# Two-layer cached-attention decode: issuing loads ahead of the projections that stood before them, and contiguous input and output transfers

## The chip, the cores and the metric

The kernel runs on one core of one Trainium2 chip. The metric is device time in microseconds (us) of that core. "Before" ran at a median of 2728.05 us over 12 runs (2727.2 to 2729.18).

## The reference, cut to what matters

```python
# B=2, one query token, D=576, H=32 heads, Dh=128, cache length Sk=16384, F=4608, all bf16
def A(x, k_cache, v_cache, wq, wo):
    q = (x @ wq).reshape(B, 1, H, Dh).transpose(0, 2, 1, 3)
    p = softmax(einsum("bhqd,bhkd->bhqk", q, k_cache) * Dh ** -0.5)
    o = einsum("bhqk,bhkd->bhqd", p, v_cache)
    return o.transpose(0, 2, 1, 3).reshape(B, 1, H * Dh) @ wo

def Bm(x, w1, w2, w3, w4):      # with S=1 the shifted half of this block is zero
    return x + gelu(layernorm(x) @ w3) @ w4

for layer in range(2):
    x = x + A(layernorm(x), K, V, wq, wo)
    x = x + Bm(layernorm(x), w1, w2, w3, w4)
```

Both layers read the same K and V cache: 64 (batch, head) units per layer, each with 4 MiB of K and 4 MiB of V. That is 1074 MB of the 1109 MB that the profile counts as read from HBM. The weights are the rest, 35 MB.

## The kernel before

The kernel streams K and V through SBUF. For a unit it transposes K tile by tile on TensorE (PE), multiplies by the unit's q, takes the exponential on ScalarE, and multiplies by V. q (`qT_sb`) of all heads is made before the units of a layer start, from the layer's normalized x and the weight wq. These are the parts that the change touches; cuts are marked.

```python
    xin = small.tile([P, NCH, B], A_x.dtype)
    xap = A_x.rearrange("b o d -> d (b o)")
    for kc in range(NCH):                     # one packet per element
        nc.sync.dma_start(xin[: rows[kc], kc, :], xap[kc * P : kc * P + rows[kc], :])
    # ... cut: cast into xT, layernorm, helpers
    xq_f, xq_bf = layernorm(xT[:])
    with tc.tile_pool(name="wq0", bufs=1) as wqpool:
        wq_sb = load_weight_chunked(wqpool, A_wq, H * Dh, tag="wq", engines=[nc.sync, nc.sync])
        qT_sb = q_projection(wq_sb, xq_bf)
    w3_sb = load_weight_chunked(const, B_w3, F, tag="w3", engines=[nc.gpsimd, nc.gpsimd])

    for layer in range(num_layers):
        with (tc.tile_pool(name=f"stream{layer}", bufs=1) as spool, ...):   # cut: six pools, per layer
            pend_k = {0: issue_k(0)}          # two DMAs of 2 MB, slots k0..k3 in turn
            pend_v = {0: issue_v(0)}          # two DMAs of 2 MB, slots v0..v3 in turn
            pend_k[1] = issue_k(1)
            for ui, (b, h) in enumerate(units):
                # issues V of unit ui+1 and K of unit ui+2, then:
                # ... cut: transposes, scores, exp, oT
            # wo in slots k0,k1,k2; w4 in k3,v0,v1; wq of the next layer in v2,v3,w0
            # ... cut: these loads, the output projection (wo), layernorm, MLP (w3, w4)
            if layer + 1 < num_layers:
                xq_f, xq_bf = layernorm(xT[:])
                # ... cut: q projection of the next layer
    xob = small.tile([P, NCH, B], out.dtype)
    nc.vector.tensor_copy(out=xob[:], in_=xT[:])
    for kc in range(NCH):                     # one packet per element
        nc.sync.dma_start(oap[kc * P : kc * P + rows[kc], :], xob[: rows[kc], kc, :])
```

The streaming pools of a layer open only after the q projection of that layer, and on memory that earlier pools held. So the first K and V of a layer wait for the q projection.

The softmax here doesn't subtract the row's maximum and nothing guards it: scores larger than these inputs give would overflow.

Of the kernel before, what the change touches and what calls it, by code (L numbers as in the profile page):

```python
# [8 lines left out]
F32 = mybir.dt.float32  # L9
BF16 = mybir.dt.bfloat16  # L10
# [7 lines left out]
def kernel(  # L18
# [40 lines left out]

    ident = const.tile([P, P], BF16)  # L60
# [6 lines left out]
    xin = small.tile([P, NCH, B], A_x.dtype)  # L67
    xap = A_x.rearrange("b o d -> d (b o)")
    with nc.allow_non_contiguous_dma(reason="tiny transposed load"):
        for kc in range(NCH):  # L70
            nc.sync.dma_start(xin[: rows[kc], kc, :], xap[kc * P : kc * P + rows[kc], :])  # L71
    for kc in range(NCH):
        nc.vector.tensor_copy(out=xT[: rows[kc], kc, :], in_=xin[: rows[kc], kc, :])
# [63 lines left out]

    xq_f, xq_bf = layernorm(xT[:])
    with tc.tile_pool(name="wq0", bufs=1) as wqpool:
        wq_sb = load_weight_chunked(wqpool, A_wq, H * Dh, tag="wq", engines=[nc.sync, nc.sync])  # L140
        qT_sb = q_projection(wq_sb, xq_bf)
    w3_sb = load_weight_chunked(const, B_w3, F, tag="w3", engines=[nc.gpsimd, nc.gpsimd])

    for layer in range(num_layers):
        R = const.tile([P, U], F32)
        oT_all = const.tile([P, U], F32)
        with (
            tc.tile_pool(name=f"stream{layer}", bufs=1) as spool,
            tc.tile_pool(name=f"kt{layer}", bufs=KT_BUFS) as ktpool,
            tc.tile_pool(name=f"sexp{layer}", bufs=2) as sexp,  # L150
            tc.tile_pool(name=f"psT{layer}", bufs=4, space=bass.MemoryType.PSUM) as psT,
            tc.tile_pool(name=f"psS{layer}", bufs=2, space=bass.MemoryType.PSUM) as psS,
            tc.tile_pool(name=f"psO{layer}", bufs=1, space=bass.MemoryType.PSUM) as psO,
        ):
            units = [(b, h) for b in range(B) for h in range(H)]
            kslot = [0]
            vslot = [0]

            def issue_k(u):
                bb, hh = units[u]  # L160
                kap = A_k_cache[bb, hh].rearrange("(p j) d -> p j d", p=P)
                tl = []
                for c in range(NKT):
                    knat = spool.tile(
                        [P, KT_J, Dh], BF16, tag=f"k{kslot[0] % KSLOTS}", bufs=1
                    )
                    kslot[0] += 1
                    nc.sync.dma_start(knat[:], kap[:, c * KT_J : (c + 1) * KT_J, :])
                    tl.append(knat)
                return tl  # L170

            def issue_v(u):
                bb, hh = units[u]
                vap = A_v_cache[bb, hh].rearrange("(p j) d -> p j d", p=P)
                tl = []
                for vc in range(NVT):
                    vt = spool.tile(
                        [P, VT_J, Dh], BF16, tag=f"v{vslot[0] % VSLOTS}", bufs=1
                    )
                    vslot[0] += 1  # L180
                    nc.sync.dma_start(vt[:], vap[:, vc * VT_J : (vc + 1) * VT_J, :])
                    tl.append(vt)
                return tl

            pend_k = {0: issue_k(0)}
            pend_v = {0: issue_v(0)}
            if len(units) > 1:
                pend_k[1] = issue_k(1)
            for ui, (b, h) in enumerate(units):
# [5 lines left out]
                if ui + 2 < len(units):  # L195
                    pend_k[ui + 2] = issue_k(ui + 2)
# [180 lines left out]
    with nc.allow_non_contiguous_dma(reason="tiny transposed store"):  # L377
        for kc in range(NCH):
            nc.sync.dma_start(oap[kc * P : kc * P + rows[kc], :], xob[: rows[kc], kc, :])
# [30 lines left out]
```

## Time and profile before

| what | before |
|---|---|
| median time | 2728.05 us |
| span of the profiled run | 2726.1 us |
| DMA rate inside both K/V streams | 428 GB/s |
| time per unit in the stream (start to start) | 20.0 us |
| first K issued | 42.75 us |
| PE start of layer 1, first unit | 1388.8 us |
| last cast of x to end of span | 20.1 us |

This is part 2 of the page of the kernel before: the span in 40 equal slices, the busy share of the 16 DMA engines in tenths (9 is 90% or more), and what they moved.

```profile
DMA  7999999999999999999879999999999999999984
GB/s 297 428 428 427 428 428 428 427 429 428 428 427 428 421 425 422 423 421 425 321 307 428 428 428 428 428 428 427 428 428 427 428 428 420 425 420 425 423 377 148
```

The DMA engines are full except at the two ends and at slices 20 and 21, the layer boundary. A kernel like this is shortened by removing DMA idle time or bytes; work on other engines counts only where it keeps DMA waiting. The next fence is the same kernel by chosen stretches. The columns are: stretch, its length, busy time of PE, weight loads, DVE, ACT and POOL, the granted PE clock, the DMA share and GB/s.

```profile
core 0: us, PE busy (x) PEld busy (x) DVE busy (x) ACT busy (x) POOL busy (x), PEclk, DMA share, GB/s
...
10.00:20.00 10.00, 0.00 (x0) 0.00 (x0) 0.34 (x2) 0.00 (x0) 0.00 (x0) 1.00 1.02 336
...
31.00:43.00 12.00, 9.89 (x156) 8.94 (x156) 0.22 (x1) 0.00 (x0) 0.00 (x0) 1.00 0.02 4
...
1363.00:1382.00 19.00, 15.09 (x276) 13.88 (x273) 2.53 (x16) 0.20 (x1) 0.00 (x0) 0.50 0.05 14
...
2686.00:2726.00 40.00, 16.61 (x343) 15.42 (x341) 2.49 (x13) 0.26 (x1) 0.00 (x0) 0.50 0.05 12
```

Three holes are seen: 12 us at the head, 19 us at the layer boundary and 40 us at the tail. In the first two no K or V moves while PE works on the q projection (in the head 156 of its matmuls, 9.9 us; at the boundary the end of the MLP comes before it). From 10 to 20 us the engines are busy and yet move only 336 GB/s. The timeline of the head (start, duration, engine, line, operation, output<-input, count, idle time before it and its releaser) shows why:

```profile
0.74 2.77 SPq L71 DMA_DIRECT2D xin<-in_A_x_dram  x5
...
20.71 0.16 DVE L73 CAST xT<-xin 64x2 f32<-64x2 bf16 x1 [2.46 <-DMA xin<-in_A_x_dram]
...
32.82 9.89 PE L127 MATMUL qT_ps<-ybf,t 64*128 64x2 bf16 x156 [2.10 <-DMA t<-in_A_wq_dram]
42.75 0.82 SPq L168 DMA_DIRECT2D knat<-in_A_k_cache_dram  x2
```

The 2.3 KB of x need 20 us to arrive, because each element is a packet of its own and these packets take turns with the large packets of w3. wq lies behind them in the same queue. K is issued after the q projection.

At the boundary and at the tail the timeline of before has:

```profile
1333.06 0.45 PE L298 MATMUL yT_ps<-oT_bf,wot 128*128 128x2 bf16 x11 [2.65 <-DMA wot<-in_A_wo_dram]
...
1336.84 0.43 PE L298 MATMUL yT_ps<-oT_bf,wot 128*128 128x2 bf16 x10 [3.33 <-DMA wot<-in_A_wo_dram]
...
1381.43 0.82 SPq L168 DMA_DIRECT2D knat<-in_A_k_cache_dram  x2
1381.44 0.23 DVE L372 CAST qT_sb<-qT_ps 128x64 bf16<-128x64 f32 x1 [10.16 <-PE qT_ps L364]
...
2706.05 0.18 DVE L375 CAST xob<-xT 128x10 bf16<-128x10 f32 x1
2706.25 2.65 SPq L379 DMA_DIRECT2D out_dram<-xob  x5
```

K of layer 1 is issued at the moment q is ready, and the span ends 20 us after the last cast. The view of DMA issues gives the store's time from issue to landing (last column):

```profile
out_dram<-xob SPq DMA_DIRECT2D x4, 0.5 KB, 17.1
```

### The profile page before, as it was taken

How to read it: one execution, taken by the hardware profiler on the slowest of the kernel's cores; microseconds unless marked ns; L12 is line 12 of the kernel's file. 1: busy time of each engine (PE TensorE's matmuls, PEld its weight loads, DVE VectorE, ACT ScalarE, POOL GpSimd, SP SyncE). 2: the span in 40 equal slices, each digit the busy share in tenths (PEclk: the TensorE clock that was granted, in tenths of full speed). 3: DMA queues.
4: the chain of work that ended last, by engine and by line, in shares of the span. 5: the costliest groups of instructions: out<-in, count | busy, mean ns of one | idle time of the engine just before them, and what ended most of it. 6: DMA issues, size and time to landing. Idle time of an engine off the chain costs nothing.

```text
span 2726.1 us, 108877 instructions
## 1 busy us (share of the span) xinstructions
PE 2334.9 (86%) x50564; PEld 2117.4 (78%) x50564; DVE 1042.6 (38%) x2268; ACT 1039.3 (38%) x2318; POOL 2.1 (0%) x8
## 2 busy tenths in 40 slices
PE   3888988889888888888779888888888988888884
PEld 3877877878778877887768877878888878887774
DVE  1343434434334343443224444343443434434341
ACT  1343443434334343443224434343443434434340
POOL 0000000000000000000000000000000000000000
PEclk9777777777777787777667877777777777878775
DMA  7999999999999999999879999999999999999984
GB/s 297 428 428 427 428 428 428 427 429 428 428 427 428 421 425 422 423 421 425 321 307 428 428 428 428 428 428 427 428 428 427 428 428 420 425 420 425 423 377 148
DMA packets 97287, 1115.54 MB, mean 409 GB/s; under 512 B 11008, under 2 KB 28416, under 8 KB 30144
## 3 DMA queue, kind: packets, MB, share of 16 engines
q1 hardware_dynamic: 96224, 1103.27, 96.0%
q8 instruction: 395, 6.47, 0.8%
q0 software_dynamic: 608, 5.31, 0.6%
q14 instruction: 60, 0.49, 0.0%
HBM read 1108.54 MB, written 0.00 MB: 407 GB/s over the span
## 4 chain that ended last, share of the span: by engine, by line
DMA 69%; PE 25%; DVE 2%; ACT 2%; issue 1%; SPq 0%; DVEq 0%
DMA knat<-in_A_k_cache_dram 67%; PE kT_ps L203 15%; PE S_ps L216 5%; PE oT_ps L243 2%; DVE ktT L208 2%; ACT ktT L210 2%; DMA t<-in_A_wq_dram 1%; DMA wot<-in_A_wo_dram 1%; PE hT_ps L316 1%; PE y_ps L342 0%; PE yT_ps L298 0%; PE qT_ps L364 0%; PE qT_ps L127 0%; ACT S_exp L230 0%; SPq L71 0%
## 5 line engine op out<-in xcount | busy, mean ns | idle before, releaser
L203 PE MATMUL kT_ps<-ident,knat 128*128 128x128 bf16 x16384 | 1628.2, 243 | 135.1 <-DMA knat<-in_A_k_cache_dram 134.7
L210 ACT COPY ktT<-kT_ps 128x384 bf16<-128x384 bf16 x2048 | 980.6, 479 | 1525.7 <-DVE ktT L208 1525.7
L208 DVE COPY ktT<-kT_ps 128x640 bf16<-128x640 bf16 x2048 | 1006.2, 492 | 881.7 <-PE kT_ps L203 775.6
L203 PEld LDWEIGHTS <-knat 128*128 128x128 bf16 x16384 | 1146.1, 108 | 143.4 <-DMA knat<-in_A_k_cache_dram 128.3
L216 PE MATMUL S_ps<-qT_sb,ktT 128*128 128x1 bf16 x16384 | 1008.9, 168 | 77.2 <-ACT ktT L210 59.1
L216 PEld LDWEIGHTS <-ktT 128*128 128x128 bf16 x16384 | 761.9, 100 | 266.6 <-ACT ktT L210 114.0
L243 PE MATMUL oT_ps<-S_exp,vt 128*128 128x1 bf16 x16384 | 459.4, 165 | 98.4 <-ACT S_exp L230 60.4
L243 PEld LDWEIGHTS <-vt 128*128 128x128 bf16 x16384 | 455.6, 102 | 112.2 <-issue 111.9
L251 DVE COPY oT_all<-oT_ps 128x1 f32<-128x1 f32 x128 | 20.3, 158 | 656.7 <-PE oT_ps L243 656.7
L230 ACT ACTIVATE S_exp<-S_ps 128x128 bf16<-128x128 f32 x128 | 35.5, 278 | 40.4 <-PE S_ps L216 40.4
L96 ACT ACTIVATE stat<-stat 1x2 f32<-1x2 f32 x4 | 0.8, 203 | 65.5 <-DVE stat L93 65.5
L230 ACT ACTIVATION_READ_ACCUMULATOR S_exp<-S_ps 128x1 f32 x128 | 24.8, 194 | 0.0
L298 PE MATMUL yT_ps<-oT_bf,wot 128*128 128x2 bf16 (+1 forms) x320 | 12.2, 170 | 14.5 <-DMA wot<-in_A_wo_dram 11.5
L316 PE MATMUL hT_ps<-ybf,t 128*128 128x2 bf16 (+1 forms) x360 | 22.7, 172 | 1.7 <-DVE ybf L110 1.7
L316 PEld LDWEIGHTS <-t 128*128 128x128 bf16 (+1 forms) x360 | 20.7, 106 | 3.7 <-issue 1.7
L298 PEld LDWEIGHTS <-wot 128*128 128x128 bf16 (+1 forms) x320 | 11.6, 114 | 15.2 <-DMA wot<-in_A_wo_dram 11.8
L81 PE MATMUL sum_ps<-x,ones_f 128*1 128x4 f32 (+1 forms) x40 | 1.8, 166 | 23.0 <-DVE x L78 23.0
L81 PEld LDWEIGHTS sum_ps<-x,ones_f 128*1 128x1 f32 (+1 forms) x40 | 1.3, 80 | 23.4 <-DVE x L78 23.2
L342 PE MATMUL y_ps<-hT_bf,w4t 128*128 128x2 bf16 (+1 forms) x360 | 12.9, 170 | 6.0 <-DVE hT_bf L337 4.0
L127 PE MATMUL qT_ps<-ybf,t 128*128 128x2 bf16 (+1 forms) x160 | 10.2, 173 | 9.1 <-DMA t<-in_A_wq_dram 9.1
L342 PEld LDWEIGHTS <-w4t 128*128 128x128 bf16 (+1 forms) x360 | 12.5, 114 | 6.4 <-issue 6.4
L127 PEld LDWEIGHTS <-t 128*128 128x128 bf16 (+1 forms) x160 | 9.1, 106 | 10.1 <-DMA t<-in_A_wq_dram 9.3
(46 smaller groups left out, 55.6 us busy)
## 6 DMA issues: line engine op xcount, KB each, us to landing
knat<-in_A_k_cache_dram SPq DMA_DIRECT2D x256, 2048.0 KB, 31.9
vt<-in_A_v_cache_dram SPq DMA_DIRECT2D x256, 2048.0 KB, 33.7
w4t<-in_B_w_dram SPq DMA_DIRECT2D x6, 1728.0 KB, 16.3
wot<-in_A_wo_dram SPq DMA_DIRECT2D x4, 1584.0 KB, 30.1
t<-in_B_w_dram POOLq DMA_DIRECT2D x1, 4608.0 KB, 16.0
t<-in_A_wq_dram SPq DMA_DIRECT2D x1, 4096.0 KB, 26.9
wot<-in_A_wo_dram SPq DMA_DIRECT2D x2, 1440.0 KB, 14.1
wqt<-in_A_wq_dram SPq DMA_DIRECT2D x2, 1408.0 KB, 15.9
```

Source lines behind the costliest of these rows:

```text
L81: nc.tensor.matmul(sum_ps[:, :], lhsT=ones_f32[: rows[kc], 0:1], rhs=x2[: rows[kc], kc, :], start=(kc == 0), stop=(kc == NCH - 1),)
L127: nc.tensor.matmul(qT_ps[:, h * B : (h + 1) * B], lhsT=wq_sb[: rows[kc], kc, h * Dh : (h + 1) * Dh], rhs=xq_bf[: rows[kc], kc, :], start=( ...
L203: nc.tensor.transpose(kT_ps[:, e, :], knats[j // KT_J][:, j % KT_J, :], ident[:])
L208: nc.vector.tensor_copy(out=ktT[:, 0:nsplit, :], in_=kT_ps[:, 0:nsplit, :])
L210: nc.scalar.copy(out=ktT[:, nsplit:EG, :], in_=kT_ps[:, nsplit:EG, :])
L216: nc.tensor.matmul(S_ps[:, j : j + 1], lhsT=ktT[:, e, :], rhs=qT_sb[:, ucol : ucol + 1], start=True, stop=True,)
L230: nc.scalar.activation(S_exp[:], S_ps[:], ACT.Exp, scale=EXP_SCALE, accum_out=R[:, ucol : ucol + 1],)
L243: nc.tensor.matmul(oT_ps[:, 0:1], lhsT=vt[:, jj, :], rhs=S_exp[:, jg : jg + 1], start=first, stop=(jg == NJ - 1),)
L251: nc.vector.tensor_copy(out=oT_all[:, ucol : ucol + 1], in_=oT_ps[:, 0:1])
L298: nc.tensor.matmul(yT_ps[: rows[c], :], lhsT=wot[:, h - h0, c * P : c * P + rows[c]], rhs=oT_bf[:, h * B : (h + 1) * B], start=(h == 0), s ...
L316: nc.tensor.matmul(hT_ps[:, g, :], lhsT=w3_sb[: rows[kc], kc, g * P : (g + 1) * P], rhs=xq2_bf[: rows[kc], kc, :], start=(kc == 0), stop=( ...
L342: nc.tensor.matmul(y2_ps[: rows[c], :], lhsT=w4t[:, g - g0, c * P : c * P + rows[c]], rhs=hT_bf[:, g, :], start=(g == 0), stop=(g == FG - 1),)
```

## The change

The intent is to let loads start as soon as their SBUF slots are free, and to move x and the output as whole rows.

- The streaming pools are opened once, before the first q projection. K0 and V0 are issued at the start; wq is loaded in three column chunks from ACT's queue into slots `v2`, `v3` and `w0`.
- wo and w4 are issued in the last unit of a layer, into slots that come free in that order.
- The next layer's K0 is issued after the output projection, V0 and K1 after the q projection in program order. SP waits only for their slots.
- x is loaded as two rows and transposed on PE; the output is transposed on PE and stored as two rows.
- A tile `pad` of 160 bytes per partition is allocated and set to zero. Nothing reads it.

```diff
+    pad = small.tile([P, 80], BF16)
+    nc.vector.memset(pad[:], 0.0)
...
-    xin = small.tile([P, NCH, B], A_x.dtype)
-        for kc in range(NCH):
-            nc.sync.dma_start(xin[: rows[kc], kc, :], xap[kc * P : kc * P + rows[kc], :])
+    xin = small.tile([B, D], A_x.dtype)
+    nc.sync.dma_start(xin[:], A_x.rearrange("b o d -> (b o) d"))
     for kc in range(NCH):
+        xin_ps = psm.tile([P, B], A_x.dtype, tag="m")
+        nc.tensor.transpose(xin_ps[...], xin[:, kc * P : ...], ident[:B, :B])
...
+    next_pend_k = {0: issue_k(0)}
+    next_pend_v = {0: issue_v(0)}
+    wq0_tags = [f"v{(NVT + i) % VSLOTS}" for i in range(NVT)] + ["w0", "w1"]
+    for i, (h0, h1) in enumerate(hgroups0):
+        t = spool.tile([P, NCH, c1 - c0], BF16, tag=wq0_tags[i], bufs=1, name=f"wq0t{i}")
+        nc.scalar.dma_start(t[:, 0:nfull, :], A_wq[0 : nfull * P, c0:c1].rearrange(...))
+        nc.scalar.dma_start(t[: rows[-1], NCH - 1, :], A_wq[(NCH - 1) * P : D, c0:c1])
...
+                if ui == nu - 1:
+                    stage_wo_w4()
...
+            if layer + 1 < num_layers:
+                next_pend_k = {0: issue_k(0)}          # after the output projection
...
+                next_pend_v = {0: issue_v(0)}          # after the q projection
+                next_pend_k[1] = issue_k(1)
...
-        for kc in range(NCH):
-            nc.sync.dma_start(oap[kc * P : kc * P + rows[kc], :], xob[: rows[kc], kc, :])
+        nc.tensor.transpose(xo_ps[:, kc, : rows[kc]], xob[...], ident[...])
+    nc.vector.tensor_copy(out=xo_sb[:], in_=...)
+    nc.sync.dma_start(out.rearrange("b o d -> (b o) d"), xo_sb[:])
```

More of the change, by code (lines that the diff above doesn't have):

```diff
@@ L66 @@
     nc.vector.memset(xT[:], 0.0)
-    xin = small.tile([P, NCH, B], A_x.dtype)
-    xap = A_x.rearrange("b o d -> d (b o)")
-    with nc.allow_non_contiguous_dma(reason="tiny transposed load"):
-        for kc in range(NCH):
-            nc.sync.dma_start(xin[: rows[kc], kc, :], xap[kc * P : kc * P + rows[kc], :])
-    for kc in range(NCH):
-        nc.vector.tensor_copy(out=xT[: rows[kc], kc, :], in_=xin[: rows[kc], kc, :])
+    xin = small.tile([B, D], A_x.dtype)
+    nc.sync.dma_start(xin[:], A_x.rearrange("b o d -> (b o) d"))
+    for kc in range(NCH):
+        xin_ps = psm.tile([P, B], A_x.dtype, tag="m")
+        nc.tensor.transpose(
+            xin_ps[: rows[kc], :], xin[:, kc * P : kc * P + rows[kc]], ident[:B, :B]
+        )
+        nc.vector.tensor_copy(out=xT[: rows[kc], kc, :], in_=xin_ps[: rows[kc], :])
     def layernorm(src, eps=1e-5):
@@ L136, in q_projection @@
         return qT_sb
-    xq_f, xq_bf = layernorm(xT[:])
-    with tc.tile_pool(name="wq0", bufs=1) as wqpool:
-        wq_sb = load_weight_chunked(wqpool, A_wq, H * Dh, tag="wq", engines=[nc.sync, nc.sync])
-        qT_sb = q_projection(wq_sb, xq_bf)
-    w3_sb = load_weight_chunked(const, B_w3, F, tag="w3", engines=[nc.gpsimd, nc.gpsimd])
+    spool = ctx.enter_context(tc.tile_pool(name="stream", bufs=1))
+    ktpool = ctx.enter_context(tc.tile_pool(name="kt", bufs=KT_BUFS))
+    sexp = ctx.enter_context(tc.tile_pool(name="sexp", bufs=2))
@@ new lines, with issue_k @@
+    psT = ctx.enter_context(tc.tile_pool(name="psT", bufs=4, space=bass.MemoryType.PSUM))
+    psS = ctx.enter_context(tc.tile_pool(name="psS", bufs=2, space=bass.MemoryType.PSUM))
+    psO = ctx.enter_context(tc.tile_pool(name="psO", bufs=1, space=bass.MemoryType.PSUM))
+    units = [(b, h) for b in range(B) for h in range(H)]
+    kslot = [0]
+    vslot = [0]
+    ktags_unit = {}
+    vtags_unit = {}
+    def issue_k(u):
+        bb, hh = units[u]
+        kap = A_k_cache[bb, hh].rearrange("(p j) d -> p j d", p=P)
+        tl = []
+        for c in range(NKT):
+            tg = f"k{kslot[0] % KSLOTS}"
+            ktags_unit.setdefault((kslot[0] // (NKT * len(units))) if False else u, []).append(tg)
+            knat = spool.tile([P, KT_J, Dh], BF16, tag=tg, bufs=1)
+            kslot[0] += 1
+            nc.sync.dma_start(knat[:], kap[:, c * KT_J : (c + 1) * KT_J, :])
+            tl.append(knat)
+        return tl
@@ new lines, in issue_v @@
+    def issue_v(u):
+        bb, hh = units[u]
+        vap = A_v_cache[bb, hh].rearrange("(p j) d -> p j d", p=P)
+        tl = []
+        for vc in range(NVT):
+            tg = f"v{vslot[0] % VSLOTS}"
+            vtags_unit.setdefault(u, []).append(tg)
+            vt = spool.tile([P, VT_J, Dh], BF16, tag=tg, bufs=1)
+            vslot[0] += 1
+            nc.sync.dma_start(vt[:], vap[:, vc * VT_J : (vc + 1) * VT_J, :])
+            tl.append(vt)
+        return tl
+    next_pend_k = {0: issue_k(0)}
@@ new lines @@
+    next_pend_v = {0: issue_v(0)}
+    HGRP0 = 11
+    hgroups0 = [(h0, min(H, h0 + HGRP0)) for h0 in range(0, H, HGRP0)]
+    wq0_tags = [f"v{(NVT + i) % VSLOTS}" for i in range(NVT)] + ["w0", "w1"]
+    wq0 = []
+    for i, (h0, h1) in enumerate(hgroups0):
+        c0, c1 = h0 * Dh, h1 * Dh
+        t = spool.tile([P, NCH, c1 - c0], BF16, tag=wq0_tags[i], bufs=1, name=f"wq0t{i}")
+        nfull = (NCH - 1) if rows[-1] != P else NCH
+        nc.scalar.dma_start(
+            t[:, 0:nfull, :], A_wq[0 : nfull * P, c0:c1].rearrange("(kc p) f -> p kc f", p=P)
+        )
+        if nfull != NCH:
+            nc.scalar.dma_start(t[: rows[-1], NCH - 1, :], A_wq[(NCH - 1) * P : D, c0:c1])
+        wq0.append((c0, c1, t))
@@ new lines @@
+    w3_sb = load_weight_chunked(const, B_w3, F, tag="w3", engines=[nc.gpsimd, nc.gpsimd])
+    xq_f, xq_bf = layernorm(xT[:])
+    qT_ps0 = psm.tile([P, U], F32, tag="m")
+    for (c0, c1, wqt) in wq0:
+        for h in range(c0 // Dh, c1 // Dh):
+            for kc in range(NCH):
+                nc.tensor.matmul(
+                    qT_ps0[:, h * B : (h + 1) * B],
+                    lhsT=wqt[: rows[kc], kc, h * Dh - c0 : (h + 1) * Dh - c0],
+                    rhs=xq_bf[: rows[kc], kc, :],
+                    start=(kc == 0),
+                    stop=(kc == NCH - 1),
+                )
@@ L144 @@
+    qT_sb = const.tile([P, U], BF16, tag="qT")
+    nc.vector.tensor_copy(out=qT_sb[:], in_=qT_ps0[:])
+    if len(units) > 1:
+        next_pend_k[1] = issue_k(1)
     for layer in range(num_layers):
@@ L146 @@
         oT_all = const.tile([P, U], F32)
-        with (
-            tc.tile_pool(name=f"stream{layer}", bufs=1) as spool,
-            tc.tile_pool(name=f"kt{layer}", bufs=KT_BUFS) as ktpool,
-            tc.tile_pool(name=f"sexp{layer}", bufs=2) as sexp,
-            tc.tile_pool(name=f"psT{layer}", bufs=4, space=bass.MemoryType.PSUM) as psT,
-            tc.tile_pool(name=f"psS{layer}", bufs=2, space=bass.MemoryType.PSUM) as psS,
-            tc.tile_pool(name=f"psO{layer}", bufs=1, space=bass.MemoryType.PSUM) as psO,
-        ):
-            units = [(b, h) for b in range(B) for h in range(H)]
-            kslot = [0]
-            vslot = [0]
-            def issue_k(u):
-                bb, hh = units[u]
-                kap = A_k_cache[bb, hh].rearrange("(p j) d -> p j d", p=P)
-                tl = []
-                for c in range(NKT):
-                    knat = spool.tile(
-                        [P, KT_J, Dh], BF16, tag=f"k{kslot[0] % KSLOTS}", bufs=1
-                    )
-                    kslot[0] += 1
-                    nc.sync.dma_start(knat[:], kap[:, c * KT_J : (c + 1) * KT_J, :])
-                    tl.append(knat)
-                return tl
-            def issue_v(u):
-                bb, hh = units[u]
-                vap = A_v_cache[bb, hh].rearrange("(p j) d -> p j d", p=P)
-                tl = []
-                for vc in range(NVT):
-                    vt = spool.tile(
-                        [P, VT_J, Dh], BF16, tag=f"v{vslot[0] % VSLOTS}", bufs=1
-                    )
-                    vslot[0] += 1
-                    nc.sync.dma_start(vt[:], vap[:, vc * VT_J : (vc + 1) * VT_J, :])
-                    tl.append(vt)
-                return tl
-            pend_k = {0: issue_k(0)}
-            pend_v = {0: issue_v(0)}
-            if len(units) > 1:
-                pend_k[1] = issue_k(1)
@@ new lines, with stage_wo_w4 @@
+        for _u in list(ktags_unit):
+            if _u > 1:
+                del ktags_unit[_u]
+        for _u in list(vtags_unit):
+            if _u > 0:
+                del vtags_unit[_u]
+        if True:
+            HGRP = 11
+            GGRP = 12
+            HGROUPS = [(h0, min(H, h0 + HGRP)) for h0 in range(0, H, HGRP)]
+            GGROUPS = [(g0, min(FG, g0 + GGRP)) for g0 in range(0, FG, GGRP)]
+            nu = len(units)
+            early_tags = []
+            wq_tags = []
+            wo_t = []
+            w4_t = []
+            def stage_wo_w4():
+                tags = ["w0"] + list(ktags_unit.get(nu - 2, [])) + list(vtags_unit.get(nu - 2, []))
+                tags += list(ktags_unit.get(nu - 1, []))
+                while len(tags) < len(HGROUPS) + len(GGROUPS):
+                    tags.append(f"x{len(tags)}")
+                wq_tags.extend(tags[len(HGROUPS) + len(GGROUPS) :] + list(vtags_unit.get(nu - 1, [])))
+                wq_tags.extend(["w1", "w2"])
+                for i, (h0, h1) in enumerate(HGROUPS):
+                    t = spool.tile([P, h1 - h0, D], BF16, tag=tags.pop(0), bufs=1, name=f"wot{i}")
+                    nc.sync.dma_start(
+                        t[:, :, :], A_wo[h0 * Dh : h1 * Dh, :].rearrange("(h d) f -> d h f", d=Dh)
+                    )
+                    wo_t.append((h0, h1, t))
+                for i, (g0, g1) in enumerate(GGROUPS):
+                    t = spool.tile([P, g1 - g0, D], BF16, tag=tags.pop(0), bufs=1, name=f"w4t{i}")
+                    nc.sync.dma_start(
+                        t[:, :, :], B_w4[g0 * P : g1 * P, :].rearrange("(g p) f -> p g f", p=P)
+                    )
+                    w4_t.append((g0, g1, t))
+            if next_pend_k is not None:
+                pend_k = next_pend_k
+                pend_v = next_pend_v
+            else:
+                pend_k = {0: issue_k(0)}
+                pend_v = {0: issue_v(0)}
+                if len(units) > 1:
+                    pend_k[1] = issue_k(1)
@@ L251 @@
                 nc.vector.tensor_copy(out=oT_all[:, ucol : ucol + 1], in_=oT_ps[:, 0:1])
-            HGRP = 11
-            GGRP = 12
-            wo_t = []
-            for i, h0 in enumerate(range(0, H, HGRP)):
-                h1 = min(H, h0 + HGRP)
-                t = spool.tile([P, h1 - h0, D], BF16, tag=f"k{i % KSLOTS}", bufs=1, name=f"wot{i}")
-                nc.sync.dma_start(
-                    t[:, :, :], A_wo[h0 * Dh : h1 * Dh, :].rearrange("(h d) f -> d h f", d=Dh)
-                )
-                wo_t.append((h0, h1, t))
-            w4_t = []
-            w4tags = [f"k{i}" for i in range(len(wo_t), KSLOTS)] + [f"v{i}" for i in range(VSLOTS)]
-            for i, g0 in enumerate(range(0, FG, GGRP)):
-                g1 = min(FG, g0 + GGRP)
-                t = spool.tile([P, g1 - g0, D], BF16, tag=w4tags[i], bufs=1, name=f"w4t{i}")
-                nc.sync.dma_start(t[:, :, :], B_w4[g0 * P : g1 * P, :].rearrange("(g p) f -> p g f", p=P))
-                w4_t.append((g0, g1, t))
             wq_next = None
             if layer + 1 < num_layers:
-                nqt = len(wo_t)
-                wqtags = (w4tags[len(w4_t) :] + [f"w{j}" for j in range(nqt)])[:nqt]
                 wq_next = []
-                for i, (h0, h1, _) in enumerate(wo_t):
+                for i, (h0, h1) in enumerate(HGROUPS):
                     c0 = h0 * Dh
                     c1 = h1 * Dh
-                    t = spool.tile([P, NCH, c1 - c0], BF16, tag=wqtags[i], bufs=1, name=f"wqt{i}")
+                    t = spool.tile(
+                        [P, NCH, c1 - c0], BF16, tag=wq_tags[i], bufs=1, name=f"wqt{i}"
+                    )
                     nfull = (NCH - 1) if rows[-1] != P else NCH
@@ L372 @@
                 nc.vector.tensor_copy(out=qT_sb[:], in_=qT_ps[:])
+                next_pend_v = {0: issue_v(0)}
+                next_pend_k[1] = issue_k(1)
     xob = small.tile([P, NCH, B], out.dtype)
     nc.vector.tensor_copy(out=xob[:], in_=xT[:])
-    oap = out.rearrange("b o d -> d (b o)")
-    with nc.allow_non_contiguous_dma(reason="tiny transposed store"):
-        for kc in range(NCH):
-            nc.sync.dma_start(oap[kc * P : kc * P + rows[kc], :], xob[: rows[kc], kc, :])
+    xo_ps = psm.tile([B, NCH, P], out.dtype, tag="m")
+    for kc in range(NCH):
+        nc.tensor.transpose(
+            xo_ps[:, kc, : rows[kc]], xob[: rows[kc], kc, :], ident[: rows[kc], : rows[kc]]
+        )
+    xo_sb = small.tile([B, D], out.dtype)
+    nc.vector.tensor_copy(
+        out=xo_sb[:], in_=xo_ps[:].rearrange("b c p -> b (c p)")[:, 0:D]
+    )
+    nc.sync.dma_start(out.rearrange("b o d -> (b o) d"), xo_sb[:])
 _INS = ['A_x', 'A_k_cache', 'A_v_cache', 'A_wq', 'A_wo', 'B_x', 'B_w1', 'B_w2', 'B_w3', 'B_w4']
```

## The prediction

> **What bounds the kernel now.** DMA, through nearly all of the span. The slice table shows the engines 90-100% busy at 428 GB/s in both K/V streams. The packet records give 19.8 us per (batch, head) unit of 8.39 MB on average; the timeline starts a unit every 20.0 us, because part of the engines finish late (at the end of each stream the DMA share falls to 0.5 for some 17 us before the last V lands). PE needs about 19.4 us where it does not wait for K, and waits for K 1.4 us per unit in layer 0 and 0.5 in layer 1 (waits view, each stream alone). What can be won is DMA idle time at three places (stretches table, timeline):
>
> - Head: first K is issued at 42.75 us, after the q projection. By then 10 MB of weights have moved, 24 us at full rate. Element-wise x loads (one packet per element) hold the SP ring until about 20 us; DMA then idles from 31 to 43.
> - Layer boundary: DMA share is near 0 from about 1363 to 1382, because K of layer 1 waits for the q projection; PE starts the unit only at 1389.1, 7.6 us after the projection.
> - Tail: five element-wise stores, issued at 2706.25, land 17 us later; the span ends at 2726.
>
> **What the change does.** Slots, not pool scopes, now order the loads. K0, V0, K1 and wq (ACT queue) are issued at the start; next-layer K0 follows the attention output projection, V0/K1 follow w4. x and output become contiguous rows plus ten tiny PE transposes and six copies (estimate 2-3 us). wq at the head moves in 2.8 KB instead of 8 KB packets (330 GB/s at the boundary, against 420: estimate +3 us).
>
> **Critical path.**
> 1. Tail: -15 us (store about 3 us instead of 17, transposes and copy about 1.5).
> 2. Boundary: -20 us of DMA idle. PE starts only 7.5 us earlier, but with K0/V0/K1 resident it runs at 19.4 instead of 20.0 us per unit until it meets the DMA limit again.
> 3. Head: ideal -14 us, but I expect only -7. The Trainium skill, "DMA: Bandwidth & Descriptors", section "Queues, rings and completion order", says each engine round-robins between queue rows by packet; in this trace 9216-byte and 2-byte packets of two queues alternated one for one from 4 to 18 us. So wq's 2.8 KB packets will alternate with 16 KB K/V packets and 9 KB w3 packets: estimate that wq completes near 60-68 us, not 30. qT comes LATER than before (about 65-70 us against 43), PE starts its first unit late, V1 (in wq's slots) and K2 (in K0's) wait, and DMA idles some 8 us. PE makes up its lateness from its slack.
>
> Staging wo/w4 gains little: their loads stay behind the last V in the same ring; the 7 us wait for wo stays.
>
> **Prediction:** 2686 us, 8 in 10 between 2674 and 2700. Faster by over 2% (below 2674): 0.09; within 2%: 0.90; slower: 0.01.
>
> **What would show it.** Head: qT copy at 60-70 us, DMA share near 1 from 3 us, a dip near 70-78. Boundary: no DMA hole at 1363-1382; first unit directly after the q projection, few K waits in the following 20 units. wo wait about 7 us still there. Tail: last store lands about 3 us after issue.
>
> **What would make it wrong.** Byte-fair arbitration (qT near 43, head -13). PE's own pace in layer 1 (it also stalls on nothing the profile names, 35 us) too near 20 us to use the boundary's lead: gain there only 8-12.

## The result, and the profile after

The kernel after runs at a median of 2683.2 us (2681.18 to 2684.23, 8 runs) against 2728.05 us. The ratio is 0.9835, 95% interval 0.9825 to 0.9845. Here and below a ratio is the mean time of one kernel's runs over that of the other's of the same rounds, so it is not quite the ratio of the medians quoted.

Part 2 of the page of the kernel after:

```profile
DMA  9999999999999999999899999999999999999995
GB/s 379 427 428 428 427 428 428 427 428 428 428 428 428 425 424 421 419 427 420 337 403 428 428 428 427 428 428 428 428 428 428 425 423 425 422 424 420 426 418 197
```

The rate inside the streams has not changed. The first slice, the boundary and the last slice have filled. By stretches, with columns as before:

```profile
10.00:20.00 10.00, 5.09 (x46) 3.76 (x47) 3.06 (x14) 0.00 (x0) 0.00 (x0) 1.00 1.02 431
...
39.00:46.00 7.00, 0.00 (x0) 0.00 (x0) 0.00 (x0) 0.00 (x0) 0.00 (x0) 1.00 1.04 269
...
60.00:80.00 20.00, 17.05 (x400) 16.15 (x398) 7.92 (x18) 8.67 (x19) 0.00 (x0) 0.97 1.01 429
...
1351.00:1370.00 19.00, 15.69 (x281) 14.55 (x279) 2.54 (x16) 0.20 (x1) 0.00 (x0) 0.50 1.01 410
...
2656.00:2681.00 25.00, 18.43 (x365) 16.80 (x364) 2.93 (x14) 0.26 (x1) 0.00 (x0) 0.50 0.07 26
```

The boundary hole is gone (410 GB/s during the q projection), the empty tail is 25 us instead of 40, and the head has no hole but a dent from 39 to 46 us. The timeline of the head after:

```profile
0.74 0.35 SPq L70 DMA_DIRECT2D xin<-in_A_x_dram  x1
1.16 0.84 SPq L163 DMA_DIRECT2D knat<-in_A_k_cache_dram  x2
...
18.96 0.80 SPq L176 DMA_DIRECT2D vt<-in_A_v_cache_dram  x2
...
24.56 28.95 SPq L163 DMA_DIRECT2D knat<-in_A_k_cache_dram  x2
...
57.80 14.14 SPq L163 DMA_DIRECT2D knat<-in_A_k_cache_dram  x2
...
62.10 0.23 DVE L210 CAST qT_sb<-qT_ps 128x64 bf16<-128x64 f32 x1 [32.55 <-PE qT_ps L202]
```

q is ready at 62.1 us, 19 us later than before, and still the kernel is faster. V0 and K1, whose slots were free from the start, go out at 19 us and at 24.6 to 53.5 us; the first piece of K2 goes out at 57.8 us. The waits of the SP queue over the first 80 us (who waited for whom, total, times, longest) name what held them:

```profile
SPq L163 <- DMA wq0t<-in_A_wq_dram: 33.1, 2, 28.3
SPq L176 <- DMA wq0t<-in_A_wq_dram: 17.0, 1, 17.0
```

K and V do not depend on wq. The trace shows these issues waiting on semaphores 100, 112 and 113, which earlier wq loads also count on: the program rotates eight semaphores over the DMAs of the SP and ACT queues, so a DMA waits until the one eight places before it has landed.

At the boundary and at the tail the timeline of after has:

```profile
1321.09 0.46 PE L357 MATMUL yT_ps<-oT_bf,wot 128*128 128x2 bf16 x11 [4.44 <-DMA wot<-in_A_wo_dram]
...
1324.80 0.42 PE L357 MATMUL yT_ps<-oT_bf,wot 128*128 128x2 bf16 x10 [3.26 <-DMA wot<-in_A_wo_dram]
...
1369.29 1.89 PE L279 MATMUL kT_ps<-ident,knat 128*128 128x128 bf16 x16
1369.39 0.23 DVE L433 CAST qT_sb<-qT_ps 128x64 bf16<-128x64 f32 x1 [10.16 <-PE qT_ps L425]
...
2677.13 0.18 DVE L438 CAST xob<-xT 128x10 bf16<-128x10 f32 x1
...
2678.60 0.28 SPq L448 DMA_DIRECT2D out_dram<-xo_sb  x1
```

PE begins the first unit of layer 1 with the end of the q projection instead of 7.4 us after it (the prediction has 7.6), the wait for wo is still there, and the span ends 3.8 us after the last cast.

### A ledger by bytes

Where a kernel is DMA-bound, its position is best told by bytes. From the trace's packet records (without instruction fetches) one can take the time at which N MB had been moved. The table gives how much earlier than in the kernel before that was, in us. It also has the experiments that it is used for below.

| MB moved | after | e3 | e5 | e6 | e9 | e10 |
|---|---|---|---|---|---|---|
| 14 (head) | 17.3 | 17.4 | 6.0 | 16.0 | 16.9 | 14.5 |
| 20 (head) | 14.1 | 12.7 | 6.0 | 13.2 | 11.1 | 14.5 |
| 40 | 13.3 | 11.6 | 5.9 | 0.5 | 9.3 | 14.6 |
| 540 (end of layer 0) | 12.9 | 11.0 | 6.2 | 0.1 | -0.9 | 14.3 |
| 566 (layer 1 streaming) | 31.1 | 15.0 | 6.6 | 19.9 | 15.3 | 34.0 |
| 1108 (all) | 29.2 | 14.6 | 6.4 | 16.4 | 0.1 | 32.2 |

For the kernel after the gain is therefore 13 us in the head, 16 to 18 at the boundary, and the rest of the 45.2 us between the two spans, 16, after the last byte. PE's own marks agree: its first transpose of the last unit of layer 0 starts at 1296.9 us (before 1310.3), that of the first unit of layer 1 at 1369.3 (1388.8), and that of the last unit of layer 1 at 2619.3 (2648.4), which is 13.3, 19.5 and 29.1 us earlier.

### The profile page after: what moved, and what is told of

It is laid out like the page before. It is cut to its first block, busy times and chain, and to the rows that moved or that the text cites. A ratio compares the mean times of both kernels' runs of the same rounds, so it can differ in the third digit from the quotient of the medians.

```text
span 2680.9 us, 108895 instructions
## 1 busy us (share of the span) xinstructions
PE 2338.5 (87%) x50574; PEld 2122.8 (79%) x50574; DVE 1042.3 (39%) x2270; ACT 1039.6 (39%) x2319; POOL 2.1 (0%) x8
## 4 chain that ended last, share of the span: by engine, by line
DMA 56%; PE 35%; ACT 3%; DVE 3%; issue 2%; ACTq 1%; another core or an unknown queue 1%; DVEq 0%
DMA knat<-in_A_k_cache_dram 55%; PE kT_ps L279 20%; PE S_ps L292 7%; PE oT_ps L319 5%; DVE ktT L284 2%; ACT ktT L286 2%; DMA wot<-in_A_wo_dram 1%; PE hT_ps L377 1%; ACTq L194 1%; ACT S_exp L306 1%; PE y_ps L403 0%; PE yT_ps L357 0%; PE qT_ps L202 0%; PE qT_ps L425 0%
## 5 line engine op out<-in xcount | busy, mean ns | idle before, releaser
L202 PE MATMUL qT_ps<-ybf,wq0t 128*128 128x2 bf16 (+1 forms) x160 | 10.4, 173 | 22.1 <-DMA wq0t<-in_A_wq_dram 22.0
L202 PEld LDWEIGHTS <-wq0t 128*128 128x128 bf16 (+1 forms) x160 | 9.2, 106 | 23.2 <-DMA wq0t<-in_A_wq_dram 22.3
L357 PEld LDWEIGHTS <-wot 128*128 128x128 bf16 (+1 forms) x320 | 11.6, 115 | 16.8 <-DMA wot<-in_A_wo_dram 13.4
L377 PEld LDWEIGHTS <-t 128*128 128x128 bf16 (+1 forms) x360 | 20.7, 106 | 3.7 <-issue 1.7
L403 PE MATMUL y_ps<-hT_bf,w4t 128*128 128x2 bf16 (+1 forms) x360 | 12.9, 170 | 6.0 <-DVE hT_bf L398 4.0
## 6 DMA issues: line engine op xcount, KB each, us to landing
wot<-in_A_wo_dram SPq DMA_DIRECT2D x2, 1440.0 KB, 14.1
wqt<-in_A_wq_dram SPq DMA_DIRECT2D x2, 1408.0 KB, 15.3
```

What stands on the lines that cost most here:

```text
L202: nc.tensor.matmul(qT_ps0[:, h * B : (h + 1) * B], lhsT=wqt[: rows[kc], kc, h * Dh - c0 : (h + 1) * Dh - c0], rhs=xq_bf[: rows[kc], kc, :] ...
L357: nc.tensor.matmul(yT_ps[: rows[c], :], lhsT=wot[:, h - h0, c * P : c * P + rows[c]], rhs=oT_bf[:, h * B : (h + 1) * B], start=(h == 0), s ...
L377: nc.tensor.matmul(hT_ps[:, g, :], lhsT=w3_sb[: rows[kc], kc, g * P : (g + 1) * P], rhs=xq2_bf[: rows[kc], kc, :], start=(kc == 0), stop=( ...
L403: nc.tensor.matmul(y2_ps[: rows[c], :], lhsT=w4t[:, g - g0, c * P : c * P + rows[c]], rhs=hT_bf[:, g, :], start=(g == 0), stop=(g == FG - 1),)
```

## The experiments

The first theory, A, was the ledger: three separate places, each worth the DMA idle time it removes, which add up. Its rivals stand with each run. Differences are against the kernel before of the same rounds; where "against after" is said, 2683.2 us is meant, which was measured in other rounds (the kernel before differs by 1 to 2 us between calls).

| run | edit | median us | before, same rounds | ratio |
|---|---|---|---|---|
| e1_store_only | before, new store only | 2711.97 | 2727.63 | 0.9943 |
| e2_load_only | before, new load of x only | 2747.37 | 2727.63 | 1.0072 |
| e3_no_boundary | after, next layer's K held | 2695.84 | 2727.63 | 0.9883 |
| e4_no_staging | after, wo/w4/wq slots as before | 2683.3 | 2727.63 | 0.9836 |
| e5_load_aligned | e2 plus a 32-byte pad | 2724.69 | 2728.57 | 0.9986 |
| e9_no_pad | after without pad | 2709.43 | 2728.57 | 0.9932 |
| e6_tails_pool | after, wq tails on POOL's queue | 2694.41 | 2728.57 | 0.9875 |
| e7_w3_late | after, w3 loaded in unit 4 | 2699.72 | 2728.57 | 0.9895 |
| e10_wq_first | after, wq ahead of K0 on SP | 2681.47 | 2730.02 | 0.9823 |
| e11_wq_first_pad_w3 | e10, w3 padded to full rows | 2676.53 | 2730.02 | 0.9804 |
| e12_pad_128 | after, pad of 48 elements | 2702.78 | 2729.52 | 0.9903 |
| e13_pad_64 | after, pad of 32 elements | 2708.84 | 2729.52 | 0.9926 |

All gave correct results.

### e1_store_only: the tail alone

```diff
 # kernel before
-        for kc in range(NCH): nc.sync.dma_start(oap[...], xob[...])
+        nc.tensor.transpose(xo_ps[...], ...)  x5;  one copy;  one contiguous dma_start
```

> The kernel before, with only the output store changed (five PE transposes, one copy, one contiguous store). Theory A (three separate places on the DMA ledger, which add): the tail is worth what the two traces show between the last cast of x and the end of the span, 20.1 us before against 3.8 us after, so about 16 us: 2712, within 2 us. Rival B (the old store's wait overlapped other end-of-kernel work, and the head and boundary carry the whole gain): 0 to 5 us, 2723 to 2728.

It measured 2711.97 us, 15.7 less than before. Theory A holds: the store is worth 16 us by itself and overlaps nothing. Here the landing of the last DMA is paid in full.

### e2_load_only: the load of x alone

```diff
 # kernel before
-        for kc in range(NCH): nc.sync.dma_start(xin[...], xap[...])
+    nc.sync.dma_start(xin[:], A_x.rearrange("b o d -> (b o) d"));  five PE transposes
```

> The kernel before, with only the load of x changed to one contiguous load and five PE transposes; K and V are still issued after the q projection, wq is still loaded in 8 KB packets behind x. Theory A: what cost time in the old head was mostly the element-wise load that held wq back until about 20 us; wq and w3 (10 MB, 24 us) now share the engines from 2 us on, the q projection ends near 31 to 33 us, K is issued there instead of at 42.75, and the whole stream moves by about 10 to 12 us: 2717 within 2. So the early issue of K and V is worth only 1 to 3 of the 13 us that the head gave. Rival B (the early issue of K and V is what pays in the head): the load alone is worth under 4 us, 2724 to 2728.

It measured 2747.37 us, 20 us slower than before. Both theories missed. In the head the trace is as theory A had it in kind: q is ready and K is issued at 35.9 us instead of 42.75, and at 14 MB the ledger is 6.8 us ahead. But the lead melts evenly, to -3.8 us at the end of layer 0 and -17.9 at the end. The stretch from 200 to 600 us, deep in the stream, of e2 and of the kernel before:

```profile
200.00:600.00 400.00, 348.77 (x7642) 316.31 (x7642) 159.00 (x338) 159.05 (x357) 0.00 (x0) 0.78 1.01 424
```

```profile
200.00:600.00 400.00, 351.00 (x7682) 318.25 (x7680) 160.10 (x341) 160.52 (x360) 0.00 (x0) 0.78 1.01 428
```

The DMA share is the same and the rate is 1% lower. In the packet records a 16 KB packet takes 611 ns in 97% of cases before, and mostly 613 to 620 ns in e2. The larger x tile had moved every later tile in SBUF. In the build before, K and V tiles start at a multiple of 256 bytes in their partition (67584 for the first K slot), in e2 192 bytes past one (69824). These addresses come from the built programs; the traces do not hold them. This pointed to the one line of the change that seemed to do nothing.

### e5_load_aligned and e9_no_pad: the start address

```diff
 # e5: kernel e2                                   # e9: kernel after
+    pad = small.tile([P, 16], BF16)               -    pad = small.tile([P, 80], BF16)
+    nc.vector.memset(pad[:], 0.0)                 -    nc.vector.memset(pad[:], 0.0)
```

> The kernel of e2 (only the load of x changed) with an unused tile of 32 bytes per partition added, so that all K and V tiles start at a multiple of 256 bytes within their partition again; in e2 they start 192 bytes past one, and a 16 KB packet takes 613 to 620 ns there instead of 611. Theory A2 (e2's loss is the start address alone, and its head gain of 6.8 us is real): 2721 within 2 us, packets at 611 ns. Rival (the loss comes from the contiguous load itself or from the earlier start): 2745 or more.

> The kernel after without its unused pad tile and the memset of it; K and V tiles then start 192 bytes past a multiple of 256 bytes. Theory A2: streaming slows as in e2, which lost 25 us over the whole span, so 2706 to 2709, and packets of 613 to 620 ns. Rival (pad does nothing, as nothing reads it): 2683 within 2 us.

e9 measured 2709.43 us: the unused pad tile is worth 26 us. Without it the ledger of e9 falls from 11.1 us at 20 MB to 0.1 at the end. Its stream, then that of the kernel after:

```profile
200.00:600.00 400.00, 359.83 (x7830) 326.94 (x7828) 164.98 (x350) 165.38 (x370) 0.00 (x0) 0.78 1.01 424
```

```profile
200.00:600.00 400.00, 364.78 (x7940) 332.18 (x7939) 164.66 (x350) 165.14 (x371) 0.00 (x0) 0.77 1.01 428
```

e5 measured 2724.69 us, with packets back at 611 ns. The address is what e2 lost by, 23 us. e5 came out 3.7 us above what was expected, outside the 2 us allowed. Its ledger keeps 6.4 us to the last byte; the rest of the gap is in the old store, which took 19.4 us to land in this trace and 17.1 in that of before. The load of x alone so gives about 6 us of the head's 13. By subtraction the early K and V give about 7; they were not tried alone.

### e12_pad_128 and e13_pad_64: which addresses are good

```diff
 # kernel after; K and V start 128 or 64 bytes past a multiple of 256
-    pad = small.tile([P, 80], BF16)
+    pad = small.tile([P, 48], BF16)      # e12; e13 has 32
```

> The kernel after with a pad of 48 instead of 80 elements: K and V tiles start 128 bytes past a multiple of 256 in their partition. Theory A2a (a start off the 256-byte grid wastes beats in proportion to the bytes before the start, 192 of them cost 26 us): two thirds of that, 2700 within 3. Theory A2b (being off the grid costs the same wherever): 2709 within 2. Rival (only some other property of the address counts, 128 is a good start): 2683.

> The kernel after with a pad of 32 elements: K and V tiles start 64 bytes past a multiple of 256. Theory A2a (in proportion): one third of the 26 us, 2692 within 3. Theory A2b (the same wherever off the grid): 2709 within 2. Rival: 2683.

e12 measured 2702.78 us and e13 2708.84. In both the rate in the stream was 424 to 425 GB/s. So 64 bytes off the grid costs as much as 192, and 128 off costs about 6 us less. e12 by itself lies inside what A2a allowed (2700 within 3) and not A2b; e13 decides against A2a, because a loss in proportion to the offset would have 64 as the mildest. A2b holds for 64 and 192; why 128 is milder stays open. (The packet records show it too: 43% of the 16 KB packets still take 611 ns in e12, 18 to 19% in e9 and e13.) The Trainium skill, "DMA: Bandwidth & Descriptors", section "How a descriptor splits into AXI transactions", says that a descriptor not starting on a 256-byte boundary needs a first transaction from the boundary below. The grid of 256 agrees with these runs. That page speaks of beats, and of reading, while here the tile that is written was moved; its beats in proportion to the offset do not explain the sizes.

### e3_no_boundary: the boundary

```diff
 # kernel after: slots so that the next layer's first K waits for the q projection
-    tags = ["w0"] + k of unit 62 + v of unit 62 + k of unit 63;  wq in k3, v2, v3
+    tags = ["w0", "v0", "v1", "k2", "k3", "v2"];                 wq in k1, v3, k0
```

> The kernel after, with the slots of the weights at the layer boundary permuted so that the first K of the next layer falls into the slot of the last wq chunk and has to wait for the end of the q projection, as before; nothing else changed. Theory A: the DMA idle hole of about 20 us comes back, PE starts its first unit some 7 us after the projection, and 16 to 18 us are lost: 2699 to 2701. Rival (PE sets the pace of layer 1, so the lead of DMA there is not used): only the immediate 6 to 7 us are lost, 2689 to 2691.

It measured 2695.84 us, 12.6 more than after and less than expected. The undo was only partial: the two K pieces were issued in the order in which their slots came free, so the first one went out at 1364.7 us, after the first wq chunk's matmuls instead of the last. The hole that came back is 13 us long:

```profile
1352.00:1365.00 13.00, 9.45 (x196) 8.81 (x194) 2.46 (x16) 0.20 (x1) 0.00 (x0) 0.50 0.07 26
```

13 us of hole cost 12.6 us of time, between the two numbers expected (16 to 18, and 6 to 7). The rival, that PE cannot use a DMA lead, falls: the kernel after keeps nearly all of its lead through layer 1 (31.1 us at 566 MB, 29.2 at the end), and e3 its smaller one (15.0 and 14.6).

### e4_no_staging: the early issue of wo and w4

```diff
 # kernel after
-    tags = ["w0"] + k of unit 62 + v of unit 62 + k of unit 63   (issued in the last unit)
+    tags = ["k0", "k1", "k2", "k3", "v0", "v1"]; wq in v2, v3, w0 (issued after the loop)
```

> The kernel after, with wo, w4 and wq given the slots and the place in the program that they had before (issued after the unit loop, wo first into the slots of K); the early K and V of the next layer stay. Theory A: wo still lies behind the last V in the same queue whatever its slot, so staging is worth nothing: 2683 within 2 us, and PE still waits 6 to 8 us for wo in each layer. Rival (the staged issue is part of the boundary gain): 5 to 10 us slower, 2688 to 2693.

It measured 2683.3 us: this part of the change is worth nothing, and PE still waits 3.5 and 3.2 us for wo in layer 0. wo lies behind the last V in the same queue whatever slot it is for.

### e6_tails_pool: no semaphore wait for V0

```diff
 # kernel after, in the head
-        nc.scalar.dma_start(t[: rows[-1], NCH - 1, :], ...)
+        nc.gpsimd.dma_start(t[: rows[-1], NCH - 1, :], ...)
```

> The kernel after with the three 64-row pieces of wq issued on the POOL queue instead of ACT's, ahead of w3. In the trace of after, V0 and K1 wait at the head for a DMA semaphore that an earlier wq load still holds (17 and 33 us), and DMA drops to 255 to 260 GB/s from 39 to 45 us. Theory A (head time is DMA time; the drop costs 3 to 4 us): V0 is issued near 3 us, the drop goes, 2679 to 2681. Rival (PE's start, not DMA, sets what the head gives): no change, 2683.

It measured 2694.41 us, 11 us slower than after; both theories missed. V0 was issued at 2 us as intended. From then on K and V packets took turns with wq's without a pause, wq's last chunk landed at 72.6 us instead of 57.4, and q was ready only at 75.9 us. V1 (in wq's slots) went out at 27.5 and 58.8 us, K2 (in K0's slots) not before 78.5, and DMA ran dry. The timeline and the stretches of e6:

```profile
78.50 7.83 SPq L163 DMA_DIRECT2D knat<-in_A_k_cache_dram  x2
```

```profile
75.92 0.23 DVE L210 CAST qT_sb<-qT_ps 128x64 bf16<-128x64 f32 x1 [52.42 <-PE qT_ps L202]
```

```profile
70.00:82.00 12.00, 9.32 (x165) 9.04 (x166) 2.99 (x7) 2.68 (x6) 0.00 (x0) 1.00 0.27 93
```

At 20 MB its ledger is 13.2 us ahead, at 40 MB 0.5. This hole lies where the prediction had placed one in the kernel after. There the accidental semaphore waits held V0 and K1 back while wq went through. But e6 differs in a second thing that was not intended. The first piece of K0 is 64 tiles, and its slot is free for K2 once PE has transposed all of them. In the kernel after all 64 transposes stand ahead of the q projection; in the build of e6 only 52 run before q is ready, and K2 waited 19.3 us for the rest. With its slot free K2's first piece (2.1 MB, 4.9 us at 428 GB/s) could have gone out after V1 at 59 us; so up to about 5 us of the 13 lost may belong to PE's order (an estimate, not tested).

### e7_w3_late: w3 out of the head

```diff
 # kernel after
-    w3_sb = load_weight_chunked(const, B_w3, F, tag="w3", engines=[nc.gpsimd, nc.gpsimd])
+                if layer == 0 and ui == 4:
+                    w3_sb = load_weight_chunked(..., engines=[nc.sync, nc.sync])
```

> The kernel after with w3 loaded from the SP queue at the fifth unit of layer 0 instead of at the start from POOL: the same bytes, moved out of the head. wq then alternates with K/V packets only. Theory A (DMA bytes in sequence count, not when qT is ready): qT is ready 10 to 17 us earlier than at 62 us, and the time stays at 2683 within 2 us. Rival (the late qT costs time, each us of it): 10 us or more faster, 2673 or less.

It measured 2699.72 us, 16 us slower. Again both missed. q was ready at 60.6 us, hardly earlier: V1, issued at 34 to 40 us, took turns with wq's last chunk. With 5.3 MB less to move in the head, DMA had moved nearly everything that it was allowed to load by 55 us. K2 went out at 64.8 us: in this build only 40 of the 64 transposes run before q is ready, and K2 waited 7.5 us for the rest. So e7 too changes PE's order, and its 16 us are not w3's alone. The stretch of e7:

```profile
55.00:65.00 10.00, 7.69 (x133) 7.35 (x134) 1.85 (x5) 1.44 (x3) 0.00 (x0) 1.00 0.03 8
```

From e6 and e7 theory A had to be sharpened (A3): when q is ready does not matter as such, but DMA can run ahead only as far as there are slots, and K2 needs PE to have transposed the first piece of K0. In the kernel after w3's 5.3 MB and the late K1 fill that time, and the transposes come early; which of these counts for how much was not tested.

### e10_wq_first: wq ahead of K

```diff
 # kernel after, in the head: the wq loads moved ahead of issue_k(0), on SP's queue
-        nc.scalar.dma_start(t[...], A_wq[...])
+        nc.sync.dma_start(t[...], A_wq[...])
```

> The kernel after with the six wq loads of the head on the SP queue ahead of K0, V0 and K1, so that K/V packets no longer alternate with them (only w3's packets on POOL's queue do). Theory A3 (the head is worth what DMA never idles; in after it idles in part from 39 to 46 us, and the runs with tails on POOL and with late w3 lost 11 and 16 us because qT came so late that K2 and V1 could not be issued before DMA ran dry): qT near 30 us, no window under 380 GB/s between 3 and 80 us, DMA some 17 us ahead of the kernel before from 20 MB on instead of 13: 2679, within 1.5. Rival (the order of the loads is neutral, the losses of those two runs have another cause): 2683 or more.

It measured 2681.47 us, between the two numbers expected, ratio 0.9823, where after had 0.9835. The intervals (0.981 to 0.9836 and 0.9825 to 0.9845) overlap, so a gain over after is not shown by the times. The ledger is 14.5 us ahead from 14 MB on, without a dent, but not the expected 17: while wq and w3 share the engines, from 20 to 30 us, they move only 342 GB/s. q was not ready near 30 us as expected but at 51.2, because PE's instruction order puts 50 transposes of K0 ahead of the q projection, and K0 now lands later (35.6 us):

```profile
41.32 9.84 PE L202 MATMUL qT_ps<-ybf,wq0t 128*128 128x2 bf16 x160
...
51.20 0.23 DVE L210 CAST qT_sb<-qT_ps 128x64 bf16<-128x64 f32 x1 [10.35 <-PE qT_ps L202]
```

### e11_wq_first_pad_w3: a version that beats both

```diff
 # e10   (cut: the load of w3 written out, the same two DMAs from POOL)
+    nc.vector.memset(w3_sb[rows[-1] :, NCH - 1, :], 0.0)
-                        lhsT=w3_sb[: rows[kc], kc, ...], rhs=xq2_bf[: rows[kc], kc, :],
+                        lhsT=w3_sb[:, kc, ...],          rhs=xq2_bf[:, kc, :],
```

> The same, and the last 64-row piece of w3 padded with zero rows to 128, so that all 180 matmuls of the MLP's first projection have 128 rows. In the traces these take 62 ns each where every fifth has 64 rows, and the 128-row, 128-column matmuls of the output projection take 31 ns. Guess: the mixture is the cause, the 180 matmuls take 5.6 us instead of 11.3, and only the tail gains by it (the boundary is DMA's): 2673.5 within 1.5. Rival (the cause is elsewhere, for example in the small accumulation groups): 2679, the 180 matmuls still 11.3 us.

It measured 2676.53 us (2673.9 to 2679.69), ratio 0.9804, interval 0.9791 to 0.9817, which lies below that of after. It overlaps that of e10, but all five runs of e11 are faster than all four of e10 in the same rounds. The guess for the time (2673.5 within 1.5) was missed by 3 us. The timeline of after, then of e11, for the 180 matmuls of the MLP's first projection in the tail:

```profile
2655.95 11.33 PE L377 MATMUL hT_ps<-ybf,t 128*128 128x2 bf16 x180 [0.87 <-DVE ybf L113]
```

```profile
2657.06 4.94 PE L382 MATMUL hT_ps<-ybf,w_sb 128*128 128x2 bf16 x180 [0.87 <-DVE ybf L113]
```

The same number of matmuls takes 4.9 us instead of 11.3 once all have 128 rows. The time fell by 4.9 us against e10, of the 6.4 that PE saved; in the two traces it fell by only 2.6, because e11's ledger is 3.6 us behind e10's at 1100 MB, which was not explained. The trace of after also shows that it is the mixture that costs: in these 180 matmuls a start follows the one before by 27 ns (median) where both have 128 rows, by 97 ns from 128 to 64 rows, and by 116 ns from 64 back to 128. The Trainium skill, "TensorEngine Tiling (Array Packing)", section "Tiling Modes", says that changing the tiling mode drains the engine and has 64 rows as a mode of its own. That would fit a cost at both changes of the row count; no run here shows the mode itself.

## Why the prediction was right or wrong

The predicted 2686 us met the measured 2683.2, but two of its three terms were off in opposite directions (head 6 us too low, boundary 2 to 4 too high), and it left out a term of 26 us that the change had taken care of. That the sum came so close is in part luck.

1. **What bounds the kernel: right.** The rate in the streams is 428 GB/s before and after, and every change of time can be put down to a change of DMA idle time, of DMA rate (e2, e9, e12, e13), or of the chain after the last byte (e1, e11).
2. **Tail, predicted -15: right.** Measured 16 us in the traces and 15.7 in e1 alone.
3. **Boundary, predicted -20: mis-sized.** The hole is gone and the ledger jumps by 18 us there, of which 16 are left at the end of the span. PE starts 6.2 us earlier relative to its place in layer 0, where 7.5 was predicted, and gains the rest by not waiting. Between 1390 and 1770 us of the kernel after, and between 1410 and 1790 of the kernel before, PE's waits for K were (total, times, longest):

```profile
PE kT_ps L279 <- DMA knat<-in_A_k_cache_dram: 2.6, 4, 1.2
```

```profile
PE kT_ps L203 <- DMA knat<-in_A_k_cache_dram: 9.6, 11, 2.2
```

4. **Head, predicted -7 with an ideal of -14: this is the step that failed.** It said "DMA idles some 8 us" near 70 to 78 us, because wq would complete "near 60-68 us" and K2 and V1 would wait. The first half held, with wq's last large piece landed at 57.4 us: packets of three queues took turns one for one. From 6 to 33 us the trace has 434 packets of 9 KB, 365 of 16 KB and 407 of 2.8 KB (by their starts). q was ready at 62.1 us, inside the 60 to 70 that the prediction asked for. The second half did not. DMA ran at 429 GB/s from 60 to 80 us. In place of that hole came the dent of 39 to 46 us, and the ledger fell from 17.3 us at 14 MB to 13.3 at 40 MB, a loss of 4 instead of 8. Two things had been overlooked. V0 and K1 were held by semaphores of wq's loads, which let wq through and left bytes for later: the second piece of K1 went out only at 53.2 us, and it and V1 kept DMA busy until 72.4. And PE's order puts all 64 transposes of K0's first piece ahead of the q projection, so K2 did not wait for q: its first piece went out at 57.8 us, 4 us before q was ready. e6 and e7, where K2 went out late, show that the predicted hole is real; both change the waits or the bytes and PE's order together, so the share of each stays open. So 13 us were gained instead of 7.
5. **wq in smaller packets, estimated +3 us: too high.** A 2816-byte packet took 112 ns, 25 GB/s for an engine, against 26.8 GB/s for a 16 KB packet: under 1 us for 4.7 MB.
6. **PE's pace without waits, predicted 19.4 us: too slow.** From unit 3 to unit 13 of the kernel after PE needed 18.8 us per unit. PE makes up a late start even faster than assumed.
7. **Staging of wo and w4, predicted to gain little: right.** PE waits 7.7 us for wo in layer 0 (4.44 and 3.26), and e4 without the staging ran at 2683.3.
8. **The pad, not mentioned: an omission.** The prediction took for granted that the rate of a stream does not depend on where its tiles lie. Had the change come without its pad, the same prediction would have been 23 us too low, outside its range.

The Trainium skill, "DMA: Bandwidth & Descriptors", section "Rules for kernel authors", says that a strided last dimension becomes one descriptor per element. The trace agrees: the 1152 elements of the output are 1152 packets of 2 bytes and took 17 us from issue to landing, and the new store with everything after it under 2.5.

## What to carry to other kernels

In a DMA-bound kernel count time in bytes moved: a lead gained in one place is kept to the end as long as there are slots to load into and no address or queue slows the stream, so each gap can be priced alone. Here the prices added: the store alone gave 15.7 of its 16 us, and 13 us of hole put back cost 12.6. Before hoisting loads, ask what they take turns with: large packets on one queue starved small ones on another (x took 20 us, wq 57). A weight that everything waits for may do better ahead of the stream in the same queue: in e10 q was ready 11 us sooner and the ledger ended 3 us further ahead, but the times do not show a gain over after. Look too at PE's order in the built program: it decides when a slot comes free, and it changed between builds. When tiles are added or resized, look at where the streamed tiles land; here 64 bytes of shift cost 1%, and a line that nothing reads was worth more than half of the whole gain.

## What the Trainium skill lacked or had wrong

- "DMA: Bandwidth & Descriptors", section "Queues, rings and completion order": it has an engine drain a packet of some 9 to 17 descriptors from a ring before switching. In these traces single packet records of two or three queues alternate one for one (from 4 to 14 us of the kernel before 390 of 2 bytes, one element each, and 406 of 9216 bytes; after 386 of the 390 a large one starts within 3 to 6 ns).
- "DMA: Bandwidth & Descriptors", section "How a descriptor splits into AXI transactions": it gives no rate for unaligned tiles. Here a 16 KB-row stream moved 428 GB/s with SBUF starts at multiples of 256 bytes, and 424 to 425 with starts 64, 128 or 192 bytes past one, 19 to 26 us of 2683; and 64 off cost more than 128 off.
- The same page, section "Specifications", gives an HBM limit of about 358 GB/s per core, and its section "Where 436 GB/s comes from" says that this binds loads from HBM. This core alone read at 428 GB/s in its streams. The page itself, under its measured rates, gives the limit for two cores that share the HBM, so only the general wording misleads.
- "TensorEngine Tiling (Array Packing)" gives no cost of mixing row counts. 180 matmuls of which every fifth had 64 rows took 11.3 us, and 4.9 us with all at 128: 97 ns from 128 to 64 rows and 116 ns back, against 27 ns without a change.
- I found on no page that a rotating set of DMA semaphores limits how many DMAs are in flight. With eight of them over the SP and ACT queues, V0 and K1 waited 17 and 33 us for unrelated loads.
